# Transposing attention probabilities by DMA from SBUF to SBUF for tiles 6 to 23 of a fused chunk attention and gated feed-forward kernel

## The chip, the cores and the metric

The kernel runs on one core of a Trainium2 chip. The metric is the device time of one execution in microseconds (us), lower is better. The kernel before was timed three times: 257.49, 254.13 and 254.38 us, with a median of 254.38 us. One more execution was recorded by the hardware profiler; it took 255.2 us, and its span from the first to the last instruction is 253.4 us.

## The reference

Chunked attention with a few memory keys, followed by a feed-forward layer with a ReLU gate. Its core, with B = 4 batches, H = 8 heads, S = 768 rows, D = 64:

```python
for c in range(nc):                                  # 24 chunks of 32 query rows
    q_c = q[:, :, c_start:c_end]
    k_full = concat([mem_k, k[:, :, l_start:r_end]]) # 8 memory keys, up to 56 context keys
    v_full = concat([mem_v, v[:, :, l_start:r_end]])
    scores = scale * matmul(q_c, k_full.T)
    a = exp(scores - max(scores))
    a = a / (sum(a) + 1e-09)
    out[:, :, c_start:c_end] = matmul(a, v_full)
x = out.transpose(0, 2, 1, 3).reshape(3072, 512)
y = (maximum(x @ w_gate, 0) * (x @ w_val)) @ w_out    # 512 -> 1536 -> 512
```

## The kernel before

**Tiles.** The 3072 rows are 24 tiles of 128 rows, six to a batch. A tile a passes through a chain of steps, each named by a short key in the planner: `t` transposes the loaded q and k on TensorE into PSUM and `tc` copies them to SBUF; `s` multiplies scores (L239); `max`, `sub`, `exp`, `sum`, `rec`, `nrm` make the probabilities, the last of them writing the SBUF tile `p_n` (L284, VectorE); `p` transposes `p_n` with four TensorE transposes of 128x128 against an identity into the PSUM tile `pT_ps` (L290), and `pc` copies that to the SBUF tile `pT` on ScalarE (L75) or VectorE (L77), whichever the planner finds free; `v` multiplies the transposed probabilities with the values in 16 small matmuls (L303), and `x` copies the result into `xT`, the feed-forward input.

**Blocks.** The feed-forward layer works on blocks of 3, 3, 4, 4, 4, 4 and 2 tiles. For block b it runs 12 steps `f`, each a gate and a value product of four matmuls (L322), with a ReLU on ScalarE (L328) and the product on VectorE (L334), and then, tile by tile, the output products `o` in groups of three matmuls (L343), a copy `oc` to an SBUF tile `o_sb` (three buffers) and a store to HBM, which SyncE issues (L350). A block's first `f` needs `xT` of all its tiles. The attention of the next block's tiles is spread over the `f` and `o` steps of the current block (a function `pace` ties a tile's start to an `f` step).

**What sets the order.** A planner inside the kernel simulates the engines with cost figures of its own, starts on every free engine the ready operation of the best priority, and writes the program in that order. Each engine then executes its instructions strictly in order, so that the order is fixed when the kernel is built and only the waits are decided on the chip. An entry of the planner names the engine and its cost, the operations that must be done (a pair adds a delay), a priority, and the buffers that it takes and gives back.

**SyncE's queue** issues DMAs in order as well: the 24 stores, and, once for each of batches 1 to 3, eight small DMAs that copy the memory rows from SBUF to SBUF (`mem_rows`, L143, 24 KB each). The semaphores of its DMAs are shared round robin by eight, so that each DMA waits until the eighth one before it has landed. GpSimd issues all large loads, with casts, on a queue of its own.

The probabilities' two steps in the planner:

```python
op(("p", a), {"PE": 0.24}, lambda e, a=a: p_t(a), [("nrm", a)], (1, a, 8), ["aps"], ["pn"])
op(("pc", a), psum(HP * 128), lambda e, a=a: p_copy(a, engine[e]), [("p", a)], (1, a, 9), ["pT"], ["aps"])
```

Of the kernel before, what the change touches and what calls it, by code (L numbers as in the profile page):

```python
# [11 lines left out]
F16 = mybir.dt.float16  # L12
# [8 lines left out]
def kernel(  # L21
# [12 lines left out]
    nc = tc.nc  # L34
# [9 lines left out]
    HP = H // 2  # L44
# [8 lines left out]
    EARLY = TPB  # L53
# [7 lines left out]
    smpool = ctx.enter_context(tc.tile_pool(name="smpool", bufs=2))  # L61
# [7 lines left out]
    aps = ctx.enter_context(tc.tile_pool(name="aps", bufs=2, space=bass.MemoryType.PSUM))  # L69
# [3 lines left out]
    def copy(eng, o, i):  # L73
        if eng is nc.scalar:
            nc.scalar.copy(o, i)  # L75
        else:
            eng.tensor_copy(o, i)  # L77
# [126 lines left out]
    P_n, PT, S_ps, SM, TMP = {}, {}, {}, {}, {}  # L204

    def qk_t(a, i):
        ps = TMP["qk", a, i] = aps.tile([128, HP, 128], BF16, tag="aps", name="qk_ps")
        x = qk_b.pop((a, i))
        for hp in range(HP):
            nc.tensor.transpose(ps[:, hp, :], x[:, 2 * hp:2 * hp + 2, :].rearrange("p h d -> p (h d)"), ident_b)  # L210

    def qk_copy(a, i, eng):
        b, t = divmod(a, TPB)
        ps = TMP.pop(("qk", a, i))
        if i == 0:
            copy(eng, qT[b][:, :, 128 * t:128 * t + 128], ps)
        else:
            o = kT[b][:, :, 4 * t:4 * t + 4, :]
            copy(eng,
                 bass.AP(tensor=o.tensor, offset=o.offset,  # L220
                         ap=[o.ap[0], [NCH * KW, HP], [KW, 4], [16 + NMEM, 2], [1, 16]]),
                 ps.rearrange("p h (c x s) -> p h c x s", c=4, x=2))

    def scores(a):
        b, t = divmod(a, TPB)
        s = sps.tile([128, 2, 512], F32, name="s_ps")
        keys = kT[b].rearrange("p h c s -> p h (c s)")
        for h2 in range(HP):
            m, par = h2 % 2, h2 // 2
            for g in range(4):  # L230
                c = 4 * t + g
                o0 = 64 * (2 * m + par)
                for r in range(2):
                    d = slice(D * r, D * r + D)
                    for k0, k1, c0 in KEY_RUNS if a < EARLY else ((0, 64, 0),):
                        k0, k1, c0 = KW * c - 16 + k0, KW * c - 16 + k1, o0 + c0 - (KW * c - 16 + k0)
                        k0, k1 = max(k0, 0), min(k1, NCH * KW)
                        if k0 < k1:
                            nc.tensor.matmul(s[CH * g:CH * g + CH, r, c0 + k0:c0 + k1],  # L239
                                             lhsT=qT[b][d, h2, CH * c:CH * c + CH],  # L240
                                             rhs=keys[d, h2, k0:k1], start=True, stop=True)
        S_ps[a] = s.rearrange("p a (h s) -> p a h s", s=64)[:, :, 0:HP, :]

    def row_max(a):
        t = a % TPB
        s4 = S_ps[a]
        if t == 0:
            nc.vector.memset(s4[0:CH, :, :, 0:16], NEG)
        if t == TPB - 1:
            e = CTX if a < EARLY else 64  # L250
            nc.vector.memset(s4[3 * CH:4 * CH, :, :, e - 8:e], NEG)
        SM[a, "mx"] = smpool.tile([128, 2, HP], F32, name="mx")
        nc.vector.reduce_max(SM[a, "mx"], s4, axis=AX.X)  # L253

    def subtract(a):
        mx = SM.pop((a, "mx"))
        SM[a, "dif"] = smpool.tile([128, 2, HP, 64], F32, name="dif")
        mx_b = bass.AP(tensor=mx.tensor, offset=mx.offset,
                       ap=[mx.ap[0], [HP, 2], [1, HP], [0, 64]])
        ps = S_ps.pop(a)  # L260
        for i0, i1, o0 in KEY_RUNS if a >= EARLY else ((0, 64, 0),):
            nc.vector.tensor_tensor(out=SM[a, "dif"][:, :, :, o0:o0 + i1 - i0], in0=ps[:, :, :, i0:i1],  # L262
                                    in1=mx_b[:, :, :, i0:i1], op=ALU.subtract)

    def exponent(a):
        p = SM[a, "p"] = smpool.tile([128, HP, 2, 64], F16, name="p_exp")
        nc.scalar.activation(p.rearrange("p (m r) a s -> p r m (a s)", r=2),  # L267
                             SM.pop((a, "dif")).rearrange("p r (m a) s -> p r m (a s)", a=2),
                             ACT.Exp, scale=SCALE)

    def row_sum(a):
        SM[a, "sm"] = smpool.tile([128, HP, 2], F32, name="sm")
        nc.vector.reduce_sum(SM[a, "sm"], SM[a, "p"], axis=AX.X)  # L273

    def reciprocal(a):
        SM[a, "rinv"] = smpool.tile([128, HP, 2], F32, name="rinv")
        nc.vector.reciprocal(SM[a, "rinv"], SM.pop((a, "sm")))

    def normalise(a):
# [3 lines left out]
        P_n[a] = smpool.tile([128, HP, 2, 64], F16, name="p_n")  # L283
        nc.vector.tensor_tensor(out=P_n[a], in0=SM.pop((a, "p")), in1=rinv_b, op=ALU.mult)  # L284

    def p_t(a):
        ps = TMP["p", a] = aps.tile([128, HP, 128], F16, tag="aps", name="pT_ps")
        x = P_n.pop(a)
        for hp in range(HP):
            nc.tensor.transpose(ps[:, hp, :], x[:, hp].rearrange("p a s -> p (a s)"), ident_h)  # L290

    def p_copy(a, eng):
        PT[a] = smpool.tile([128, HP, 128], F16, name="pT", bufs=6)
        copy(eng, PT[a], TMP.pop(("p", a)))
# [67 lines left out]
    def op(key, eng, fn, deps=(), prio=(0,), take=(), give=(), after=()):  # L362
        ops[key] = dict(eng=eng, fn=fn, deps=list(deps), prio=prio, take=list(take), give=list(give),
                        after=list(after))
# [4 lines left out]
    def psum(n):  # L369
        return {"ACT": 0.21 + 0.83e-3 * n, "DVE": 0.22 + 1.04e-3 * n}  # L370

    engine = {"ACT": nc.scalar, "DVE": nc.vector}
# [22 lines left out]
    def pace(a):  # L395
        blk = block_of[a]
        return [("f", blk - 1, NDC * (a - starts[blk]) // BLOCKS[blk], 0)] if blk > 1 else []

    for a in range(NT):
        b, t = divmod(a, TPB)  # L400
        last = t == TPB - 1
        for i in (1, 0):
            op(("t", a, i), {"PE": 0.24}, lambda e, a=a, i=i: qk_t(a, i), [("qk", a, i), "ib", ("new", b)],
               (1, a - i, 0), ["aps"], ["qk"], pace(max(a - i, 0)))
            op(("tc", a, i), psum(HP * 128), lambda e, a=a, i=i: qk_copy(a, i, engine[e]), [("t", a, i)],
               (1, a - i, 0), (), ["aps"])
        op(("s", a), {"PE": 0.8 if a < EARLY else 0.36}, lambda e, a=a: scores(a),
           [("tc", a, 0), ("tc", a, 1)] + ([] if last else [("tc", a + 1, 1)]), (1, a, 1), ["sps"],
           ["kv"] if last else [], [("s", a - 1)] if a else [])
        op(("max", a), {"DVE": 0.74 + (0.2 if t == 0 or last else 0)}, lambda e, a=a: row_max(a), [("s", a)],  # L410
           (1, a, 2), ["mx"])
        op(("sub", a), {"DVE": 0.74 if a < EARLY else 1.2}, lambda e, a=a: subtract(a), [("max", a)],
           (1, a, 3), ["dif"], ["sps", "mx"])
        op(("exp", a), {"ACT": 0.66}, lambda e, a=a: exponent(a), [("sub", a)], (1, a, 4), ["p"], ["dif"])
        op(("sum", a), {"DVE": 0.74}, lambda e, a=a: row_sum(a), [("exp", a)], (1, a, 5), ["sm"])
        op(("rec", a), {"DVE": 0.24}, lambda e, a=a: reciprocal(a), [("sum", a)], (1, a, 6), ["rinv"], ["sm"])
        op(("nrm", a), {"DVE": 0.74}, lambda e, a=a: normalise(a), [("rec", a)], (1, a, 7), ["pn"], ["p", "rinv"])
        op(("p", a), {"PE": 0.24}, lambda e, a=a: p_t(a), [("nrm", a)], (1, a, 8), ["aps"], ["pn"])
        op(("pc", a), psum(HP * 128), lambda e, a=a: p_copy(a, engine[e]), [("p", a)], (1, a, 9), ["pT"], ["aps"])
        blk = block_of[a]  # L420
        j = a - starts[blk]
        op(("v", a), {"PE": 0.45}, lambda e, a=a: values(a),
           [("pc", a)] + [("vl", b, 0 if b else t // 3, n) for n in range(2 if b else 2 * HP)]
           + ([("mr", b)] if b else []), (1, a, 10), ["aps"] + (["xT"] if j == 0 else []), ["pT"],
           [("v", a - 1)] if a else [])
        op(("x", a), psum(HP * 128), lambda e, a=a: x_copy(a, engine[e]), [("v", a)], (1, a, 11), (), ["aps"],
           [("x", a - 1)] if a else [])
# [6 lines left out]
    for rank, (blk, m) in enumerate(seq):  # L434
        n = BLOCKS[blk]
# [212 lines left out]
```

## Time and profile before

| What | us | Where it is read |
|---|---|---|
| median of three runs | 254.38 | times |
| profiled execution, its span | 255.2, 253.4 | times, page |
| PE busy, of the span | 231.7 (91%) | page, part 1 |
| `f` products of value and gate, busy | 76.2 and 76.5 | page, part 5, L322 |
| output products, busy | 66.1 | page, part 5, L343 |
| probability transposes, 96 of them for 24 tiles, busy | 10.3 | groups by line, L290 |
| copies of `pT`: 15 on ScalarE of 0.585, 9 on VectorE of 0.424 | 8.8 and 3.8 | groups by line, L75 and L77 |
| first gate product of blocks 2, 3, 4, 5, 6 starts at | 89.70, 126.62, 163.52, 200.27, 233.96 | chain that ended last |

A busy figure of PE adds overlapping matmuls with modelled ends; how much of PE's line an operation takes is better read from the chain, where one piece starts when the one before it leaves the engine. The granted TensorE clock is 0.999 over the span. The DMA engines carry GpSimd's loads until about 130 us (the DMA row of the slices is at 9 there) and are almost idle later, but for the stores.

### The profile page before, as it was taken

The page shows a single profiled execution, that of the slowest core. Times are in us where ns is not written, and L with a number is a line of the kernel's source. Part 1 is how long each engine was busy: PE and PEld are TensorE (multiplying, and loading weights), DVE is VectorE, ACT ScalarE, POOL GpSimd, SP SyncE. Part 2 cuts the span into 40 slices and gives each one's busy share as a digit, 9 for nine tenths or more (in the row PEclk, how much of TensorE's full clock was granted, in tenths as well). Part 3 has the DMA queues.
Part 4 walks back from the last instruction along what each step waited for, and adds up shares of the span by engine and source line. Part 5 has one row for each costly group of instructions (what it writes and reads, how often), then busy time and mean ns, then how long its engine had stood idle before and what let it go on. Part 6 is the DMA issues. An engine that isn't in the chain of part 4 may idle for free.

```text
span 253.4 us, 6546 instructions
## 1 busy us (share of the span) xinstructions
PE 231.7 (91%) x2785; PEld 129.9 (51%) x2785; DVE 142.0 (56%) x295; ACT 107.1 (42%) x197; POOL 89.7 (35%) x102
## 2 busy tenths in 40 slices
PE   1628777999999999999999999999999999999993
PEld 0417555666654544554545555544545545454861
DVE  3957664567764247775257775168774075810430
ACT  3426444445454244543253554354434434332421
POOL 8999699993335644597010000000000000000000
PEclk9999999999999999999999999999999999999999
DMA  8999999999999999999991001210002200002102
GB/s 63 113 113 132 164 148 175 160 144 192 145 151 158 201 180 151 152 136 109 181 192 23 0 3 41 87 41 3 3 1 83 85 0 3 0 27 101 41 3 83
DMA packets 115053, 23.99 MB, mean 95 GB/s; under 512 B 106320, under 2 KB 111952, under 8 KB 115024
## 3 DMA queue, kind: packets, MB, share of 16 engines
q0 software_dynamic: 106400, 16.61, 89.2%
q1 hardware_dynamic: 8624, 6.97, 9.7%
q8 instruction: 22, 0.36, 0.6%
q14 instruction: 7, 0.06, 0.1%
HBM read 33.24 MB, written 6.29 MB: 156 GB/s over the span
## 4 chain that ended last, share of the span: by engine, by line
PE 77%; POOL 9%; DMA 8%; SPq 2%; issue 2%; ACT 1%; POOLq 0%; ACTq 0%
PE v_ps L322 24%; PE g_ps L322 24%; PE out_ps L343 21%; POOL v_bd L167 4%; POOL qk_b L189 4%; PE qk_ps L210 3%; DMA w_val_sb<-in_moe_w_val_dram 3%; DMA w_gate_sb<-in_moe_w_gate_dram 3%; PE xT_ps L303 2%; DMA out_dram<-o_sb 2%; SPq L143 2%; PE s_ps L239 2%; PE pT_ps L290 1%; POOL w_gate_sb L101 0%; ACT o_sb L75 0%
## 5 line engine op out<-in xcount | busy, mean ns | idle before, releaser
L322 PE MATMUL v_ps<-xT,w_val_sb 128*128 128x512 f16 (+2 forms) x336 | 76.2, 349 | 0.9 <-DMA w_val_sb<-in_moe_w_val_dram 0.9
L322 PE MATMUL g_ps<-xT,w_gate_sb 128*128 128x512 f16 (+2 forms) x336 | 76.5, 351 | 0.3 <-ACT xT L75 0.3
L328 ACT ACTIVATE g_relu<-g_ps 128x512 f16<-128x512 f32 (+2 forms) x84 | 45.0, 536 | 73.2 <-PE g_ps L322 63.7
L334 DVE TENSOR_TENSOR gvT<-v_ps,g_relu 128x512 f16<-128x512 f32 (+2 forms) x84 | 51.6, 614 | 42.7 <-PE v_ps L322 29.3
L343 PE MATMUL out_ps<-w_out_sb,gvT 128*128 128x512 f16 x288 | 66.1, 379 | 0.0
L322 PEld LDWEIGHTS <-w_gate_sb 128*128 128x128 f16 x336 | 32.5, 98 | 29.2 <-issue 1.2
L322 PEld LDWEIGHTS <-w_val_sb 128*128 128x128 f16 x336 | 30.6, 98 | 22.9 <-issue 1.4
L343 PEld LDWEIGHTS <-gvT 128*128 128x128 f16 x288 | 26.8, 98 | 28.7
L167 POOL DMA_DIRECT2D v_bd<-in_v_dram x24 | 27.9, 1182 | 11.3 <-issue 8.7
L75 ACT COPY o_sb<-out_ps 128x512 f32<-128x512 f32 x24 | 14.1, 586 | 34.3 <-PE out_ps L343 31.0
L189 POOL DMA_DIRECT2D qk_b<-in_k_dram x24 | 22.8, 949 | 14.9 <-PE v_ps L322 4.0
L210 PE MATMUL qk_ps<-ident_b,qk_b 128*128 128x128 bf16 x192 | 19.9, 241 | 8.2 <-DMA qk_b<-in_q_dram 6.1
L189 POOL DMA_DIRECT2D qk_b<-in_q_dram x24 | 22.5, 940 | 13.0 <-PE qk_ps L210 9.0
L210 PEld LDWEIGHTS <-qk_b 128*128 128x128 bf16 x192 | 14.2, 106 | 13.2 <-DMA qk_b<-in_q_dram 6.7
L273 DVE TENSOR_REDUCE sm<-p_exp 128x8 f32<-128x512 f16 x24 | 16.3, 679 | 7.6 <-ACT p_exp L267 7.4
L253 DVE TENSOR_REDUCE mx<-s_ps 128x8 f32<-128x512 f32 x24 | 16.4, 685 | 7.2 <-PE s_ps L239 6.9
L262 DVE TENSOR_TENSOR dif<-s_ps,mx 128x256 f32<-128x256 f32 (+3 forms) x60 | 18.7, 362 | 0.2
L267 ACT ACTIVATE p_exp<-dif 128x512 f16<-128x512 f32 x24 | 15.2, 632 | 4.8 <-DVE dif L262 4.7
L284 DVE TENSOR_TENSOR p_n<-p_exp,rinv 128x512 f16<-128x512 f16 x24 | 16.5, 687 | 0.4
L77 DVE COPY qT<-qk_ps 128x512 bf16<-128x512 bf16 x9 | 3.8, 424 | 21.2 <-PE qk_ps L210 21.2
L303 PEld LDWEIGHTS <-v_bd 128*128 128x128 f16 x384 | 12.9, 97 | 4.4 <-issue 0.8
L75 ACT CAST xT<-xT_ps 128x512 f16<-128x512 f32 x18 | 10.5, 586 | 9.4 <-PE xT_ps L303 9.3
(37 smaller groups left out, 126.4 us busy)
## 6 DMA issues: line engine op xcount, KB each, us to landing
out_dram<-o_sb SPq DMA_DIRECT2D x24, 256.0 KB
v_bd<-in_v_dram POOLq DMA_DIRECT2D x5, 672.0 KB, 16.3
qk_b<-in_k_dram POOLq DMA_DIRECT2D x24, 128.0 KB, 8.0
qk_b<-in_q_dram POOLq DMA_DIRECT2D x24, 128.0 KB, 7.5
w_gate_sb<-in_moe_w_gate_dram POOLq DMA_DIRECT2D x8, 192.0 KB, 6.1
w_val_sb<-in_moe_w_val_dram POOLq DMA_DIRECT2D x8, 192.0 KB, 6.7
w_out_sb<-in_moe_w_out_dram POOLq DMA_DIRECT2D x2, 768.0 KB, 11.7
v_bd<-in_v_dram POOLq DMA_DIRECT2D x15, 84.0 KB, 4.7
```

The lines of the kernel that those rows point to most:

```text
L75: nc.scalar.copy(o, i)
L167: nc.gpsimd.dma_start(dst[64 * par + s0:64 * par + s1, c0:c1, D * par:D * par + D], bass.AP(tensor=v.tensor, offset=v[b, HP * par, 0, 0].o ...
L189: nc.gpsimd.dma_start(qk_b[a, i], bass.AP(tensor=x.tensor, offset=x[b, 0, 128 * t, 0].offset, ap=[[D, 128], [S * D, H], [1, D]]))
L210: nc.tensor.transpose(ps[:, hp, :], x[:, 2 * hp:2 * hp + 2, :].rearrange("p h d -> p (h d)"), ident_b)
L253: nc.vector.reduce_max(SM[a, "mx"], s4, axis=AX.X)
L262: nc.vector.tensor_tensor(out=SM[a, "dif"][:, :, :, o0:o0 + i1 - i0], in0=ps[:, :, :, i0:i1], in1=mx_b[:, :, :, i0:i1], op=ALU.subtract)
L284: nc.vector.tensor_tensor(out=P_n[a], in0=SM.pop((a, "p")), in1=rinv_b, op=ALU.mult)
L303: nc.tensor.matmul(ps[:, hp, r], lhsT=v_bd[b % NSET][:, hp, 4 * t + g, :], rhs=x[:, hp, r], start=True, stop=True)
L322: nc.tensor.matmul(ps, lhsT=w[:, f, 128 * m:128 * m + 128], rhs=xTs[blk][:, f, :], start=(f == 0), stop=(f == NFC - 1))
L328: nc.scalar.activation(st["r", m], st.pop((0, m)), ACT.Relu)
L334: nc.vector.tensor_tensor(out=st["gv"][:, m, :], in0=st.pop((1, m)), in1=st.pop(("r", m)), op=ALU.mult)
L343: nc.tensor.matmul(st["o", t], lhsT=st["gv"][:, m, 128 * t:128 * t + 128], rhs=w_out_sb[:, m, :], start=(m == 0), stop=(m == NDC - 1))
```

## The change

For tiles 6 to 23 the two steps are replaced by one, `pc` on SyncE's queue: four DMAs with transposition, each from one 128x128 quarter of `p_n` to the same quarter of `pT`. Tiles 0 to 5 (`EARLY` is 6) keep TensorE and the copy. The planner is given 3.0 us of SyncE's time for the four and a delay of 2.5 us before `v`. The PSUM buffer `pT_ps` is no longer taken by these tiles, and `p_n` is held until the DMAs are done.

```diff
+    def p_dma(a):
+        PT[a] = smpool.tile([128, HP, 128], F16, name="pT", bufs=6)
+        x = P_n.pop(a)
+        for hp in range(HP):
+            nc.sync.dma_start(PT[a][:, hp, :], x[:, hp].rearrange("p a s -> p (a s)"), transpose=True)
+
...
-        op(("p", a), {"PE": 0.24}, lambda e, a=a: p_t(a), [("nrm", a)], (1, a, 8), ["aps"], ["pn"])
-        op(("pc", a), psum(HP * 128), lambda e, a=a: p_copy(a, engine[e]), [("p", a)], (1, a, 9), ["pT"], ["aps"])
+        if a < EARLY:
+            op(("p", a), {"PE": 0.24}, lambda e, a=a: p_t(a), [("nrm", a)], (1, a, 8), ["aps"], ["pn"])
+            op(("pc", a), psum(HP * 128), lambda e, a=a: p_copy(a, engine[e]), [("p", a)], (1, a, 9), ["pT"], ["aps"])
+        else:
+            op(("pc", a), {"SP": 3.0}, lambda e, a=a: p_dma(a), [("nrm", a)], (1, a, 8), ["pT"], ["pn"])
...
-           [("pc", a)] + [("vl", b, 0 if b else t // 3, n) for n in range(2 if b else 2 * HP)]
+           [("pc", a) if a < EARLY else (("pc", a), 2.5)] + [("vl", b, 0 if b else t // 3, n) for n in range(2 if b else 2 * HP)]
```

Since the planner decides the order of all engines, the new costs move other instructions too.

## The prediction

> **What bounds the kernel now.** The page comes first: who is busy, and which chain ended last.
>
> ```profile
> PE 231.7 (91%) x2785; PEld 129.9 (51%) x2785; DVE 142.0 (56%) x295; ACT 107.1 (42%) x197; POOL 89.7 (35%) x102
> ...
> PE 77%; POOL 9%; DMA 8%; SPq 2%; issue 2%; ACT 1%; POOLq 0%; ACTq 0%
> ```
>
> Three quarters of the chain are PE, the rest mostly the loads of the first 40 us. The busy times by stretch, cut at the first gate product of each block, show how full PE is (columns: stretch, length, then busy us of PE, PEld, DVE, ACT, POOL, the clock, DMA share, GB/s):
>
> ```profile
> 90.00:126.60 36.60, 36.60 (x384) 18.62 (x383) 23.03 (x50) 15.19 (x28) 19.56 (x18) 1.00 2.11 150
> 126.60:163.50 36.90, 36.88 (x386) 18.98 (x385) 22.48 (x48) 16.81 (x30) 0.87 (x1) 1.00 0.40 60
> ```
>
> PE has no free time here, at the full clock, so only what leaves PE's line can shorten these stretches, and any wait of PE lengthens them. The eighteen copies that go were ScalarE's and VectorE's, busy 15 to 23 us of 37: no gain. The timeline at the end of block 2, with tile 13, the last one block 3 needs:
>
> ```profile
> 114.58 0.31 PE L239 MATMUL s_ps<-kT,qT 64*32 64x64 bf16 x32
> ...
> 114.82 3.41 PE L343 MATMUL out_ps<-w_out_sb,gvT 128*128 128x512 f16 x15
> ...
> 121.43 0.68 DVE L284 TENSOR_TENSOR p_n<-p_exp,rinv 128x512 f16<-128x512 f16 x1
> 123.22 0.39 PE L290 MATMUL pT_ps<-ident_h,p_n 128*128 128x128 f16 x4
> ...
> 123.45 2.11 PE L343 MATMUL out_ps<-w_out_sb,gvT 128*128 128x512 f16 x9
> ...
> 125.39 0.56 PE L303 MATMUL xT_ps<-pT,v_bd 128*128 128x32 f16 x16
> 125.79 0.81 PE L343 MATMUL out_ps<-w_out_sb,gvT 128*128 128x512 f16 x3
> 125.98 0.59 ACT L75 CAST xT<-xT_ps 128x512 f16<-128x512 f32 x1 [1.97 <-PE xT_ps L303]
> 126.62 0.59 PE L322 MATMUL g_ps<-xT,w_gate_sb 128*128 128x512 f16 x2
> ```
>
> Read start against start: four transposes hold PE from 123.22 to 123.45, 0.23 us; `v` holds it 0.40; from the end of `v` to the gate product that needs its copy, 126.62 - 125.79 = 0.83 us pass, and three output matmuls (0.65) cover them.
>
> The third place is SyncE's queue, the transposes' new home. The timeline of that queue, the chain after it, the durations of its two kinds of issue (min, median, max in ns) and its wait at the very end:
>
> ```profile
> 51.78 11.26 SPq L143 DMA_DIRECT2D v_bd<-vmem  x8
> ```
> ```profile
> 75.23 7.31 SPq L143 DMA_DIRECT2D v_bd<-vmem  x8
> ```
> ```profile
> 82.64 5.84 DMA out_dram<-o_sb
> ...
> 88.58 0.59 ACT o_sb L75
> 89.16 0.50 ACT xT L75
> ...
> 89.70 1.02 PE g_ps L322 x4
> ```
> ```profile
> L143 SPq DMA_DIRECT2D v_bd<-vmem x24: 685/718/3779, 51.8 to 134.0; - x24
> ```
> ```profile
> L350 SPq DMA_DIRECT2D out_dram<-o_sb x24: 332/333/519, 74.7 to 250.3; - x24
> ```
> ```profile
> SPq L643 <- DMA out_dram<-o_sb: 1.4, 1, 1.4
> ```
>
> A store issued at 82.64, beside the loads, lands at 88.48: 5.4 us after its 0.48 of issue. The last store, beside nothing, lands 1.4 us after its issue. Block 2 already starts late through this queue.
>
> **What leaves PE.** 18 tiles x 0.23 = 4.1 us. That is the whole possible gain: 1.6% of the profiled 255.2 us. About 2%, 5.1 us, is what a measurement of this kernel can tell from no change, so even the full gain would be below it.
>
> **What the new order takes back.** In the built program of the changed kernel `v` of tiles 9, 13, 17 and 21, the last of their blocks, is PE's last work before the next block's gate product; the three matmuls that stood behind it are ahead of it. So the copy's 0.83 us are bare, once for each of blocks 2 to 5. Against the four transposes saved per block (0.92), a block gains 0.1. Only the last two tiles keep theirs, 0.45.
>
> **What a DMA transpose costs.** No row shows one. The leg from `p_n` to `v` is L = 4i + r + 0.1, with i the issue of one on SyncE, r the landing, 0.1 the signal. For i the nearest rows are the store, 0.33 (128 partitions, 2 KB each), and the memory rows, also SBUF to SBUF in small pieces, 0.72 at the median; under the heaviest load eight of these took 11.26, 1.41 each. I take 0.70, the small-piece row, with 0.33 and 1.41 as ends. For r the ends are 1.4 and 5.4; with the DMA engines idle (after 130 us, tile 14 on) I take 1.4, beside the loads (tiles 8 to 13) the middle, 3.4. So L is 4.3 late and 6.3 early.
>
> [...]
>
> **What L may be.** PE work between `s` and `v` of a tile in the changed order, less the time that the chain from `s` to the end of `p_n` takes now, is free for L:
> - Tile 13: 16 groups of three output matmuls (0.648) and two `v`: 11.2, less 122.11 - 114.82 = 7.3: 3.9 us.
> - Tile 21, the same work, less 194.14 - 188.49 = 5.6: 5.5 us. Tile 17: two `f` and a `v` more, 13.3 less 6.7: 6.6 us.
> - The others from tile 10 on, with 12.7 to 19 us of work ahead and chains of 6 to 9.3: 5.1 (tile 20) to about 11 (tile 14), mostly 7. Tiles 6 and 7 wait over 15 us for `v` already.
> - `p_n` has two buffers, now held for L instead of the transposes' 0.2: the next but one `nrm` on VectorE waits for it only where two tiles come within L; inside a block they are over 6 us apart (p_n at 100.8, 107.3, 116.0, 121.4), so this costs nothing while L stays below that.
>
> **Block 2.** Tiles 8 and 9 go behind the memory rows, which leave SyncE at 82.54. The order there is: store, store, tile 8's four, store, tile 9's four. By issue alone tile 9 is out at 82.54 + 0.9 + 2.8 + 0.5 + 2.8 = 89.5. But the second of its four shares the semaphore of the store issued at 82.64, and waits for its landing at 88.48: 88.5 + 3 x 0.70 = 90.6. Landing 3.4 and signal 0.1: 94.1. `v` and the bare copy, 1.23: block 2 starts at 95.3, not 89.70: +5.6. Between the ends of i and r: +2.5 to +9.7. Queued behind these DMAs are two more stores, whose `o_sb` buffers ScalarE waits for; they come in the same stretch.
>
> **The sum.** Block 2 +5.6; block 3: tile 13 exceeds its room by 6.3 - 3.9 = 2.4, less 0.1: +2.3; blocks 4 and 5, L 4.3 below 5.1: -0.1 each; the last two tiles -0.45. Together +7.3 us: 255.2 + 7.3 = 262.5 for a profiled execution, which stood 0.8 above the median, so 262 as a time. With both low ends it is 2.5 - 0.3 - 0.45 = +1.8. With both high ends, L 11.1 early and 7.1 late: block 2 +9.7, tiles 10 to 12 some 4, tile 13 some 7, tiles 16 to 22 together some 6, less 0.8: +26.
>
> **Rivals.**
> - Likeliest, 0.42: i between 0.5 and 1.05, as summed: 260 to 266 us.
> - Not slower (0.29): the transposes do not queue behind the loads, r stays 1.4 at tiles 8 to 13. Then with i = 0.70 block 2 starts at 88.5 + 2.1 + 1.5 + 1.23 = 93.3, +3.6, tile 13 is 0.4 over, and the sum is +3.3; with i = 0.33 it is +1.8: 256 to 258 us. It decides below r = 2.3, where +3.3 + 2 x 0.9 reaches 5.1. For it: SBUF-to-SBUF, no HBM at either end. Against: the same 16 engines carry GpSimd's loads, and the memory rows' max of 3.78 us is such a queue.
> - The transposes' issue is SyncE's bound (0.27): i from 1.05 to 1.41 and above. Then L is over 5.7 even late, tiles 20 and 21 and then others wait too, each us of L costs several: 266 to 281 us. For it: a transposing DMA is many small pieces. Against: with engines idle no row of SyncE reaches it.
> - Faster by over 2% (0.02): 4.1 us is all there is on PE.
> - That the change does not do what it says is excluded: the built program has 72 transposing DMAs on SyncE, and PE 144 rows fewer.
>
> **Numbers.** The likeliest gives 262 us. The range takes in all three, 255 to 281, leaving about 0.07 above (a slower i) and 0.05 below. Slower by over 2% (259.5): the third and most of the first, 0.66; within 2%: the second and the edge of the first, 0.32; faster 0.02.
>
> **What will show it.** The issue rows of the transposes on SyncE give i at once; waits of `xT_ps` on `pT`'s DMAs, and their place, give L against its room: at tiles 9 and 13 alone if I am right, at inner tiles if the third rival is, nearly none if the second. Every block's first gate product should wait about 0.8 us for its `xT` copy. I am wrong if blocks 4 and 5 lengthen beyond 37 us, or if block 2 starts before 92 us.

## The result and the profile after

The changed kernel takes 287.69 us (median of 4 runs, 285.02 to 288.75) beside 255.94 for the kernel before (4 runs, 254.13 to 257.72): a ratio of 1.127, 95% interval 1.121 to 1.133. It is slower, as forecast, but 26 us slower than the forecast and 7 us outside the range. Here and below a time is the median of all executions, while a ratio leaves out those that took over 1.5% longer than the fastest of the same kernel. The profiled execution took 288.75 with a span of 286.9, against 255.2 and 253.4 before. The page of the changed kernel, its busy times, the granted clock over the span, and the chain that ended last:

```profile
PE 239.5 (83%) x2713; PEld 130.2 (45%) x2713; DVE 136.8 (48%) x282; ACT 105.1 (37%) x192; POOL 89.9 (31%) x102
...
PEclk9999988999999558999957899999999999999999
...
PE 69%; DMA 11%; SPq 8%; POOL 4%; issue 3%; ACT 3%; DVE 1%; DVEq 0%; ACTq 0%; POOLq 0%
```

Two things are to be seen. SyncE's queue and DMAs have grown to a fifth of the chain. And PE is busy 7.8 us longer than before with 72 rows fewer; the clock line has two holes, down to 5 tenths, and the longer busy time lies in the stretches with these holes. Mean granted clock: 0.940, before 0.999. The stretches from one block's first gate product to the next (stretch, length, busy us of PE, PEld, DVE, ACT, POOL, clock, DMA share, GB/s; the first row is the lateness of block 2):

```profile
89.70:103.80 14.10, 2.77 (x35) 1.59 (x34) 1.69 (x2) 2.25 (x4) 7.07 (x5) 0.59 1.78 160
103.80:155.50 51.70, 41.25 (x368) 19.68 (x368) 21.67 (x47) 15.48 (x27) 14.68 (x14) 0.86 1.60 111
155.50:196.50 41.00, 38.83 (x369) 19.09 (x369) 21.05 (x45) 16.34 (x29) 0.88 (x1) 0.94 0.20 42
```

Before, blocks 2 to 6 began at 89.70, 126.62, 163.52, 200.27 and 233.96; now at 103.83, 155.50, 196.47, 234.07 and 267.47. So the 33.5 us by which the span grew are: 14.1 ahead of block 2, 14.8 in block 2 (51.7 for 36.9), 4.1 in block 3, 0.9 in block 4, -0.3 in block 5, nothing after it. Of the 14.1 not all is the change's: block 1's first gate product is already 2.5 us late, before and after,

```profile
53.08 0.65 PE g_ps L322 x4
```
```profile
55.62 0.65 PE g_ps L328 x4
```

although PE's instructions have the same order in both kernels up to here and the first transposing DMA is issued at 64.3. In the other runs below, block 1 starts between 1 us earlier and 2 us later than before, so this is a difference between executions. 11.6 of the 14.1 belong to the change. PE's own waits name the cause (total us, times, longest):

```profile
PE xT_ps L309 <- DMA pT<-p_n: 22.4, 15, 5.7
...
PE g_ps L328 <- ACT xT L75: 2.7, 4, 0.7
```

The second row is the bare copy, four times 0.67 us. The first is the transposing DMA. The longest of its waits are not only at the last tiles of a block: tile 8 waits 6.0 us in four pieces and tile 12 7.0 in two, beside 4.7 at tile 9 and 2.7 at tile 13. The longest piece of tile 8's and of tile 12's in the timeline (in brackets the wait):

```profile
94.16 0.29 PE L309 MATMUL xT_ps<-pT,v_bd 128*128 128x32 f16 x4 [3.88 <-DMA pT<-p_n]
```
```profile
145.78 0.27 PE L309 MATMUL xT_ps<-pT,v_bd 128*128 128x32 f16 x4 [5.65 <-DMA pT<-p_n]
```

What SyncE pays to issue one (min, median, max in ns; first and last start):

```profile
L290 SPq DMA_TRANSPOSE pT<-p_n x72: 1093/1230/3105, 64.3 to 258.4; - x72
```

Not 0.70 us but 1.23, and never below 1.09. The chain at tile 9, ahead of block 2 (start, length, what):

```profile
92.02 1.10 SPq L290
...
95.89 6.95 DMA pT<-p_n
102.89 0.28 PE xT_ps L309 x4
103.19 0.59 ACT xT L75
103.83 1.87 PE g_ps L328 x4
```

Tile 9's four issues take SyncE from 92.02 to 97.13, 5.1 us, as tile 8's did before them (86.17 to 91.29). The last lands at 102.84, 5.7 us after its issue. Then come `v`, the bare copy, and a gate product that takes 1.87 us where it took 1.02 before. The same chain at tiles 12 and 13, ahead of block 3:

```profile
132.13 0.61 DVE p_n L284
132.79 1.09 SPq L290
...
135.21 3.10 SPq L290
138.36 2.83 SPq L290
...
142.80 2.63 SPq L290
...
146.75 7.50 DMA pT<-p_n
154.30 0.55 PE xT_ps L309 x8
...
155.50 1.87 PE g_ps L328 x4
```

`p_n` of tile 12 is ready at 132.7 and that of tile 13 at 136.9, 4.2 us later, less than four issues take. Some issues take 2.6 to 3.1 us here, and two stores stand between. So tile 13 waits 5.9 us for its first issue, and its leg from `p_n` to the last landing is 17.3 us; it had been given 6.3, and had 3.9 of room. What else happens there shows on GpSimd's queue: the value loads of batch 3, in the timeline after and then before (`no_v_loads` below tests whether they are the reason),

```profile
132.63 4.97 POOL L167 DMA_DIRECT2D v_bd<-in_v_dram  x3 [10.82 <-PE xT_ps L309]
```
```profile
112.31 2.21 POOL L167 DMA_DIRECT2D v_bd<-in_v_dram  x1 [0.26 <-PE qk_ps L210]
```

These loads wait until `v` of tile 11 frees their buffer (the bracket: 10.82 us of idling, ended by `xT_ps`). `v(11)` does not wait for its transposes; it ends 28.3 us after block 2's first gate product instead of 22.1, since the new order has it later, and block 2 starts 14 us late. So the loads are issued at 132.6 instead of 112.3, 0.16 us ahead of tile 12's transposes.

The clock holes lie at and behind the two long waits:

```profile
90.30:103.80 13.50, 2.19 (x32) 1.50 (x33) 1.69 (x2) 2.25 (x4) 6.91 (x5) 0.58 1.83 160
103.80:109.40 5.60, 5.57 (x20) 2.48 (x19) 1.12 (x2) 1.18 (x2) 1.20 (x2) 0.50 2.56 147
```

PE idles for most of 13.5 us, and the next 5.6 us, in which it never waits, run at half clock, 2.8 us lost; from 109.4 on it is 1.00 again. Behind block 3's wait the same goes from 155.5 to 160.6, some 2.5 us.

### The profile page after: what moved, and what is told of

Read it like the earlier page. It is cut to its first block, busy times and chain, and to the rows that moved or that the text cites. A ratio compares the mean times of both kernels' runs of the same rounds, so it can differ in the third digit from the quotient of the medians.

```text
span 286.9 us, 6498 instructions
## 1 busy us (share of the span) xinstructions
PE 239.5 (83%) x2713; PEld 130.2 (45%) x2713; DVE 136.8 (48%) x282; ACT 105.1 (37%) x192; POOL 89.9 (31%) x102
## 3 DMA queue, kind: packets, MB, share of 16 engines
q1 hardware_dynamic: 20144, 9.33, 13.9%
## 4 chain that ended last, share of the span: by engine, by line
PE 69%; DMA 11%; SPq 8%; POOL 4%; issue 3%; ACT 3%; DVE 1%; DVEq 0%; ACTq 0%; POOLq 0%
PE g_ps L328 24%; PE v_ps L328 23%; PE out_ps L349 13%; SPq L290 8%; DMA pT<-p_n 7%; PE qk_ps L210 4%; PE s_ps L239 3%; POOL qk_b L189 2%; PE xT_ps L309 2%; DMA out_dram<-o_sb 2%; DMA qk_b<-in_q_dram 2%; POOL v_bd L167 1%; ACT xT L75 1%; ACT o_sb L75 1%; PE pT_ps L296 1%
## 5 line engine op out<-in xcount | busy, mean ns | idle before, releaser
L328 PE MATMUL g_ps<-xT,w_gate_sb 128*128 128x512 f16 (+2 forms) x336 | 80.3, 363 | 4.0 <-ACT xT L75 2.7
L328 PE MATMUL v_ps<-xT,w_val_sb 128*128 128x512 f16 (+2 forms) x336 | 78.5, 357 | 0.0
L328 PEld LDWEIGHTS <-w_gate_sb 128*128 128x128 f16 x336 | 33.2, 101 | 32.5 <-issue 7.3
L328 PEld LDWEIGHTS <-w_val_sb 128*128 128x128 f16 x336 | 31.8, 100 | 24.4 <-issue 1.8
L349 PEld LDWEIGHTS <-gvT 128*128 128x128 f16 x288 | 27.5, 99 | 31.8 <-issue 1.9
L309 PE MATMUL xT_ps<-pT,v_bd 128*128 128x32 f16 x384 | 16.0, 180 | 23.2 <-DMA pT<-p_n 22.4
L75 ACT COPY o_sb<-out_ps 128x512 f32<-128x512 f32 x24 | 14.1, 586 | 42.4 <-PE out_ps L349 35.6
L309 PEld LDWEIGHTS <-v_bd 128*128 128x128 f16 x384 | 14.1, 98 | 29.1 <-issue 17.2
L75 ACT CAST xT<-xT_ps 128x512 f16<-128x512 f32 x20 | 11.7, 586 | 35.1 <-PE xT_ps L309 35.0
L210 PEld LDWEIGHTS <-qk_b 128*128 128x128 bf16 x192 | 15.2, 111 | 15.7 <-DMA qk_b<-in_q_dram 6.7
L273 DVE TENSOR_REDUCE sm<-p_exp 128x8 f32<-128x512 f16 x24 | 16.3, 680 | 10.4 <-ACT p_exp L267 10.3
```

The source lines that it names most:

```text
L309: nc.tensor.matmul(ps[:, hp, r], lhsT=v_bd[b % NSET][:, hp, 4 * t + g, :], rhs=x[:, hp, r], start=True, stop=True)
L328: nc.tensor.matmul(ps, lhsT=w[:, f, 128 * m:128 * m + 128], rhs=xTs[blk][:, f, :], start=(f == 0), stop=(f == NFC - 1))
L349: nc.tensor.matmul(st["o", t], lhsT=st["gv"][:, m, 128 * t:128 * t + 128], rhs=w_out_sb[:, m, :], start=(m == 0), stop=(m == NDC - 1))
```

## The experiments

The theory after this result, A: the price is SyncE's issue of 1.23 us per DMA, and the rest follows from it, since (so I thought) block 2's lateness moves GpSimd's loads onto tiles 12 and 13. Its rivals, B: the landing beside loads (5 to 6 us) is the price, whatever the issue; C: the order of stores and transposes in SyncE's queue; D: the planner, which reserves 3.0 us of SyncE and a delay of 2.5 for a leg that takes 6 and more, puts `v` too early on PE; E: the clock. Ratios are to the kernel before, run on the same chip, whose medians were 255.3 to 256.6 us. Every diff is against the changed kernel, and `...` stands for lines left out.

**Which tiles cost it.** `late_only` leaves tiles 6 to 13 to TensorE, `early_only` tiles 14 to 23:

```diff
-        if a < EARLY:
+        if a < 14:                      # late_only
+        if a < EARLY or a >= 14:        # early_only
```

> DMA transposes for tiles 14 to 23 alone; 6 to 13 go back to TensorE and a copy. If the loss comes from the early tiles, whose transposes land behind GpSimd's loads (and from the clock that falls in the waits they cause), blocks 2 and 3 start where they did before and only some 3 us are left: 256 to 260 us, clock 1.0. If the issue of 1.23 us each on SyncE is what costs, loaded or not, ten of eighteen tiles keep their share, some 18 of 33 us: about 273.

> The other part: DMA transposes for tiles 6 to 13, TensorE for 14 to 23. If the early tiles are the loss: 282 to 288 us, block 2 about 14 late, block 3 about 29, nothing added behind it. If the issue is the loss in every tile: about 15 us, 270.

`late_only`: 261.89 us, ratio 1.028 (0.995 to 1.060), between the two times expected. Blocks 2 and 3 start nearly as before, at 90.95 and 127.87; block 3 takes 40.3 us, since tile 17 waits 3.1, and block 4 38.6, whose first 4.2 us have a granted clock of 0.59. `early_only`: 284.41, ratio 1.116 (1.083 to 1.149), blocks 2 and 3 at 103.43 and 153.84. So most of the loss comes with tiles 6 to 13, those beside GpSimd's loads; the ten late ones cost some 5 us, an amount that the interval does not tell from nothing, and gain nothing, although little but the stores is on the DMA engines there (42, 37 and 44 GB/s in blocks 3, 4 and 5 of the changed kernel, 111 in block 2). Tile 17 in the changed kernel shows why:

```profile
189.47 1.11 SPq L290
...
193.18 2.33 DMA pT<-p_n
195.55 0.27 PE xT_ps L309 x4
```

Less the issue of 1.23 the last DMA lands in 1.1 us. But the first of the four goes out 1.9 us after `p_n` is ready (187.6), behind tile 16's and two stores, and four issues then make the leg long enough for PE to stand there.

**Issue or landing.** `half` sends only two of the four quarters through DMAs, the others through TensorE and a copy of half the size; `halves` cuts every DMA into two of 64 rows; `one_dma` sends all four quarters in one:

```diff
-        for hp in range(HP):
+        for hp in range(2):             # half, and for the other two:
...
+            nc.tensor.transpose(ps[:, hp, :], x[:, 2 + hp].rearrange("p a s -> p (a s)"), ident_h)
...
+        copy(eng, PT[a][:, 2:4, :], TMP.pop(("p", a)))
...
-            nc.sync.dma_start(PT[a][:, hp, :], x[:, hp].rearrange("p a s -> p (a s)"), transpose=True)
+            for r in (0, 64):           # halves
+                nc.sync.dma_start(PT[a][:, hp, r:r + 64], x[r:r + 64, hp].rearrange("p a s -> p (a s)"), transpose=True)
+        nc.sync.dma_start(PT[a], x.rearrange("p h a s -> p (h a s)"), transpose=True)   # one_dma
```

> Of each tile from 6 on, two quarters go by DMA and two by TensorE and a copy of half the size. The leg has two issues less, 2.5 us; the landing behind the loads is the same. If the issues carry the loss, block 2 starts some 7 us earlier than with four (tiles 8 and 9 stand one behind the other) and block 3 some 10 to 14: 262 to 268 us. If the landing behind the loads carries it, with 5.8 us whatever the number, less is won: 275 to 280.

> Each transposing DMA is cut into two of 64 rows, so a tile has eight. If the issue of 1.23 us goes with the size, eight take about as long as four did, and the time is 287 to 297. If it is a cost of each DMA, whatever its size, a tile takes 9.8 us of SyncE, and eighteen tiles add about 5 us each to the leg, most of it bare: over 340.

> One transposing DMA for the whole tile (128 rows of 512) in place of four of 128 columns. If the issue's 1.23 us is a price of each DMA, whatever its size, a tile takes 1.2 us of SyncE instead of 4.9, and the loss falls to some 10 to 20 us, what the landing behind the loads and the bare copies cost: 265 to 275. If it is a price of each 128x128 block, one DMA holds SyncE about as long as four: 285 to 290.

`half`: 277.91 us, 1.091 (1.058 to 1.123), on the landing's side of what was expected: block 2 starts at 95.89, 8 us earlier than with four (5.2 earlier counted from block 1's first gate product, near the four issues of 1.23 saved at tiles 8 and 9), but its stretch is still 50.6 us. `halves`: 371.26 (one run); PE waits 76.3 us for `pT` in 55 waits. `one_dma`: 273.20, 1.066 (1.058 to 1.074). The issue rows of the last two, `halves` first:

```profile
L291 SPq DMA_TRANSPOSE pT<-p_n x144: 1089/1226/3831, 62.2 to 339.2; - x144
```
```profile
L289 SPq DMA_TRANSPOSE pT<-p_n x18: 1189/1196/3480, 62.0 to 238.8; - x18
```

Half the rows, 1.23 us; one quarter, 1.23 (above); four quarters, 1.20. For these three sizes the issue is a price per DMA and not per byte, row or 128x128 block. With it cut to a quarter, 14.5 us come back (287.69 - 273.20), but almost 18 stay (273.20 beside 255.43). A is right about a part of block 2's delay: counted from block 1, block 2 starts 6.2 us earlier, about half of the 11.6. The rest is there with one issue too, as tile 9's single DMA shows, 1.3 us of issue and 6.5 of landing, and so does tile 13's, which takes 11 us, 3.5 of issue and 7.6 of landing:

```profile
86.14 7.74 DMA pT<-p_n
...
129.46 11.05 DMA pT<-p_n
140.56 0.62 PE xT_ps L308 x16
```

It also shows that the lateness of block 2 is not what brings the loads to tile 13: block 2 starts 8.6 us earlier here, the loads go out at 124.3 and 126.5, and tile 13's DMA still meets them. They are released by `v(11)`, just ahead of tile 12's `p_n` in this order, wherever the block begins.

**The loads.** `no_v_loads` leaves out the four value loads of batches 2 and 3 (tiles 12 to 23 then use old values); `v_loads_later` was to hold them back until `v` of tiles 9 and 13:

```diff
-            load_v_op(b, 0, par, 0, HP * NCH, par, [], deps)
+            if b < NSET:                # no_v_loads
+                load_v_op(b, 0, par, 0, HP * NCH, par, [], deps)
+            else:
+                load(("vl", b, 0, par), 0, 0.0, lambda: None, [], (), deps)
+            load_v_op(b, 0, par, 0, HP * NCH, par, [("v", {2: 9, 3: 13}[b])] if b >= NSET else [], deps)   # v_loads_later
```

> The changed kernel without GpSimd's four large loads of values for batches 2 and 3 (672 KB each; the values of batches 0 and 1 stay in their place, so the output of tiles 12 to 23 is other than the reference). In the changed kernel two of them are issued when tile 9's transposes go out and two with tile 12's. If the transposes' landing queues behind these, tiles 12 and 13 land some 2 us after their issue instead of 4.6 to 6.2, the stretch of block 2 falls from 51.7 us to about 40, and block 2 starts some 3 us earlier: 268 to 275 us in all. If a transpose's landing is long early for another reason (the number in flight, SyncE's own stores and memory rows): over 282.

> The same four loads are kept but issued later: for batch 2 after tile 9's values, for batch 3 after tile 13's. If it is a matter of which transfers lie before the transposes in time, tile 13's leg shortens as without the loads, and block 2's stretch falls by about 10 us; batch 2's loads may now meet tiles 10 and 11, whose room is 7 us: 272 to 280. If the loads are no cause: 285 to 290.

`no_v_loads`: 275.03 us, 1.079 (1.056 to 1.100). Block 2 starts at 101.55, hardly earlier, but its stretch falls from 51.7 to 41.2, and tile 13's last DMA goes as a late one does:

```profile
138.15 1.23 SPq L290
139.43 2.38 DMA pT<-p_n
```

No issue of tiles 12 and 13 takes over 1.3 us, and the last lands 1.15 after its own: the loads were what made both slow at tiles 12 and 13. Tile 9's landing stays slow, 5.4 us after its last issue, beside GpSimd's loads of q and k, which are still there. `v_loads_later` says nothing: 287.71 us, 1.128 (1.112 to 1.145), because the edit moved only a time in the planner; GpSimd's queue kept its order and issued batch 3's loads at 132.6 as before.

With the loads left out on top of `one_dma`:

> One DMA for a tile and no large loads of values for batches 2 and 3 (output of tiles 12 to 23 other than the reference, as before). If the number of DMAs and these loads are separate prices, both gains show, 14.5 and 12.7 of 33 us: 259 to 263, with block 3 starting 37 us after block 2, and what is left is tiles 8 and 9 behind SyncE's memory rows and stores. If they are one and the same wait seen twice: 268 to 273.

263.53 us, 1.034 (1.027 to 1.041). The two prices add up nearly: 14.5 and 12.7 us apart, 24.2 together. The time is just above the 259 to 263 expected, and block 3 starts 38.5 us after block 2, not 37. Of the 8 us that are left, 6.5 are ahead of block 2 (96.25 for 89.70), where tile 9's DMA goes out at 86.42, 6.3 us after `p_n`, behind the memory rows and stores, and lands 8.5 us later, 7.2 after its issue. So B's price, the landing beside loads, is what is left there, with the place in the queue.

**The order on SyncE.** `stores_act` lets ScalarE issue the output's stores:

```diff
-        nc.sync.dma_start(out[row:row + 128, :], o)
+        nc.scalar.dma_start(out[row:row + 128, :], o)
```

> The 24 stores are issued by ScalarE instead of SyncE, so tile 9's transposes stand behind tile 8's alone and share no semaphores with stores. If waiting in SyncE's queue carries part of the loss, block 2 starts 3 to 4 us earlier, tile 13's transposes go out 1.5 us earlier, tile 17's and 21's 1 us: 280 to 284. If the queue's order costs nothing: 286 to 289, or more, since ScalarE now issues and waits.

290.31 us, 1.139 (1.117 to 1.160): no gain. The eight issues of tiles 8 and 9 start at 86.94, right behind the memory rows, which end later here; the first of tile 9 starts at 93.15 (92.02 before the edit), though no store of the queue stands ahead of it, and block 2 at 108.0. The chain holds a wait that the changed kernel did not have:

```profile
93.99 6.03 DMA out_dram<-o_sb
...
100.04 6.97 DMA pT<-p_n
```

Tile 9's last DMA, which could have started at 96.8, is held until a store of ScalarE's has landed at 100.02, 3.2 us. That is the kind of wait that I had forecast for SyncE's store. Without it block 2 would have started at about 104.8, no earlier than the 103.83 of the changed kernel, whose block 1 had begun 2 us later. So this run has nothing for C: moving the stores out of the queue does not bring tile 9 out sooner.

**The planner.** `planner_told` gives it 5.0 us of SyncE for a tile and a delay of 6.0 (1.5 from tile 14 on):

```diff
-            op(("pc", a), {"SP": 3.0}, lambda e, a=a: p_dma(a), [("nrm", a)], (1, a, 8), ["pT"], ["pn"])
+            op(("pc", a), {"SP": 5.0}, lambda e, a=a: p_dma(a), [("nrm", a)], (1, a, 8), ["pT"], ["pn"])
...
-            [("pc", a) if a < EARLY else (("pc", a), 2.5)] + [("vl", b, 0 if b else t // 3, n) for n in range(2 if b else 2 * HP)]
+            [("pc", a) if a < EARLY else (("pc", a), (1.5 if a >= 14 else 6.0))] + [("vl", b, 0 if b else t // 3, n) for n in range(2 if b else 2 * HP)]
...
```

> Four DMAs as in the change, but the planner is told what they take: 5.0 us of SyncE, and 1.5 us of delay before the values late, 6.0 early. If the loss came from the planner's too small figures (3.0 and 2.5), which place the values ahead of their data, it puts other work there and the time falls to 265 to 275. If the work to fill the time with is not there, since the last tile of a block is needed by the next block's first product, it only moves the waits: 283 to 290.

285.68 us, 1.115 (1.106 to 1.123), and PE still waits 24.1 us for `pT`. D is worth some 2 us, and its interval touches the changed kernel's (1.121 to 1.133): telling the planner the measured leg does not remove the waits.

**The clock.** `filler` puts 81 gate-shaped matmuls on PE around the waits of tiles 8, 9, 12 and 13, some between the quarters of `v`, so the earlier quarters of these four tiles are overwritten. `one_filler` does it for `one_dma`, 51 matmuls ahead of the first quarter:

```diff
+    FILL = {8: (16, 4, 3, 0), 9: (10, 3, 3, 2), 12: (24, 5, 0, 0), 13: (4, 7, 0, 0)}   # filler, ahead of quarter hp
...
+            for _ in range(FILL.get(a, (0, 0, 0, 0))[hp]):
...
+        for _ in range({8: 13, 9: 10, 13: 28}.get(a, 0)):                               # one_filler
+            nc.tensor.matmul(ps.rearrange("p h s -> p (h s)"), lhsT=w_gate_sb[:, 0, 0:128], rhs=w_val_sb[:, 0, 0:512],
+                             start=True, stop=True)
```

> The changed kernel with 81 more matmuls, of 0.22 us each, in the places where TensorE waits for the transposes of tiles 8, 9, 12 and 13 (into the PSUM tile that the values then overwrite; their results are not used). They fill the waits and are no longer than these. If the fall of the granted clock after the waits is a cost of its own, it stays at 1.0, the first products of blocks 2 and 3 take 0.86 instead of 1.87, and some 5 us are won: 281 to 284. If the clock does not hang on TensorE's idling, or costs nothing, the time stays at 286 to 289 or grows.

> One DMA for a tile, and 51 more matmuls of 0.22 us ahead of the values of tiles 8, 9 and 13, where TensorE waits for 3.1, 2.5 and 6.6 us; the values overwrite what they write. If the clock falls because TensorE idles there, it stays at 1.0, block 3's stretch falls from 39.5 to 37 us, and the time from 273 to 269 to 271. If the clock falls for another reason: 273 or more, with the clock down about 10 us after tile 13's wait as before.

`filler`: 291.45 us, 1.144 (1.105 to 1.182). The clock stays at 1.0 as far as 195 us and block 3's stretch falls from 41.0 to 38.8, but block 2's does not (52.8), since tile 13's transposes, which land at 152.8 and later as in the changed kernel, set its end and not PE. Later blocks lose: block 4 takes 40.5 for 37.6, and begins with 3.5 us at a granted clock of 0.51. On the total it decides nothing. `one_filler`: 270.21, 1.061 (1.054 to 1.067), beside 273.20 (1.058 to 1.074): the intervals overlap, and the reading rests on the windows. The first 5.6 us of block 3, in `one_dma` and then in `one_filler`:

```profile
141.80:147.40 5.60, 5.56 (x20) 2.47 (x19) 1.12 (x2) 1.18 (x2) 0.88 (x1) 0.50 1.72 146
```
```profile
141.80:147.40 5.60, 5.60 (x63) 2.76 (x63) 3.08 (x7) 1.98 (x4) 0.88 (x1) 1.00 1.91 159
```

Both start the block at 141.8. With PE kept busy through its wait, these 5.6 us hold 63 matmuls instead of 20, at the full clock, and the block takes 36.8 us instead of 39.5. So E is a part of the loss: this wait of PE costs its length and then 2.8 us more.

**A version without waits.** If the explanation holds, DMA transposes where the leg has room, with tiles 17 and 21 left to TensorE, must keep TensorE's saving and lose nothing. `inner_late` has four DMAs a tile for tiles 14 to 23 without 17 and 21, `one_inner` one DMA for the inner tiles from 6 on, `one_room` one DMA for tiles 10, 11 and the late inner ones; in each the planner is told the measured leg:

```diff
-        if a < EARLY:
+        if a < 14 or a in (17, 21):                         # inner_late, SP 5.0, delay 1.5
+        if a < EARLY or a in (8, 9, 12, 13, 17, 21):        # one_inner, SP 2.0, delay 5.0, from tile 14 on 2.0
+        if a < 10 or a in (12, 13, 17, 21):                 # one_room, SP 2.0, delay 2.0
...
```

> The four DMAs only where the profile has room for them: tiles 14 to 23 without 17 and 21, which end a block; the planner is told 5.0 and 1.5 us. Eight tiles x 0.23 us leave TensorE, no wait of it for a transpose should be over 0.5 us, no block waits for a bare copy: 1 to 2 us faster than before, ratio 0.992 to 0.998. If a transposing DMA disturbs TensorE's work otherwise, or the room is too small, the ratio is over 1.

> One DMA for a tile, and only where there is room: tiles 6, 7, 10, 11, 14, 15, 16, 18, 19, 20, 22 and 23; TensorE for those that end a block, and for 8 and 12, which go out beside the large loads. The planner is told 2.0 us of SyncE, and 5.0 (early) or 2.0 of delay. If a transpose in the room is free, 12 x 0.23 us leave TensorE: 2 to 3 us faster than before, ratio 0.988 to 0.993. If tiles 10 and 11 meet loads and wait, or planning moves more than it saves: 0.995 or more.

> One DMA for a tile, for tiles 10, 11, 14, 15, 16, 18, 19, 20, 22 and 23; tiles 6 and 7 are back on TensorE, so that the order up to block 2's first product is that of the kernel before. If the order around the stores was what cost 4 us there, block 2 starts at about 89.7 as before and ten tiles save 0.23 each: ratio 0.985 to 0.995, blocks 2, 3 and 4 about 36.1 us each. If the transposes of tiles 10 and 11 cost what the others save: 0.997 or more.

`inner_late`: 254.36 us (10 runs), ratio 0.995 (0.990 to 0.999): faster than the kernel before by half a per cent, with an interval that just leaves out 1. The trace shows where. PE waits for no `pT` at all, and blocks 3 and 4 take 36.1 us where they took 36.90 and 36.75; block 3:

```profile
126.60:162.70 36.10, 36.08 (x373) 18.14 (x372) 21.75 (x46) 16.34 (x29) 0.88 (x1) 1.00 0.46 72
```

The two blocks together gain 1.5 us for six tiles, 0.25 a tile. `one_inner`: 257.57, 1.010 (1.004 to 1.016), a miss: the later blocks take 36.3, 36.1 and 36.1, but block 2 starts at 94.05. Its chain there:

```profile
83.11 5.80 DMA out_dram<-o_sb
89.02 0.59 ACT o_sb L75
...
90.14 0.58 PE xT_ps L308 x16
```

With other costs in its plan the planner put a copy into `o_sb` on ScalarE, which waits 5.6 us for a store to land, ahead of two copies of `xT`, one of which PE then waits 3.0 us for. `one_room`, in which block 2 starts at 88.96, removes that loss but not more: 256.69 (12 runs), 0.995 (0.990 to 1.001), not told from no change. Tile 10, beside loads, waits 1.8 us, and the clock falls after it (the 3.4 us around the wait, then the next 3.4):

```profile
105.70:109.10 3.40, 1.61 (x23) 0.78 (x21) 1.63 (x5) 1.13 (x2) 0.00 (x0) 1.00 2.46 125
109.10:112.50 3.40, 3.40 (x16) 1.76 (x15) 1.42 (x4) 1.27 (x4) 3.07 (x4) 0.51 3.02 128
```

So block 2 takes 39.9 us instead of 36.9 and loses more than the 2.0 us that blocks 3 to 5 win.

## Why the forecast was wrong

- **The step that failed first is "What a DMA transpose costs".** I took i = 0.70 from the memory rows as small pieces between SBUF and SBUF; it measures 1.23, nearly four store issues. `halves` and `one_dma` show that it is a price per DMA. The third rival had i right, 1.05 to 1.41, at a chance of 0.27; its time, up to 281 us, was still too low. The many small pieces that it went by are there, 160 packets of some 205 bytes for each of the 72 DMAs (the hardware queue carried 20,144 packets and 9.33 MB, before 8,624 and 6.97), but the issue did not follow the size. The argument against it, that with engines idle no row of SyncE reached it, was no evidence: SyncE had issued no such DMA. With no load beside them issue and landing together take 2.3 us (tile 17): the landing, 1.1, is near the last store's 1.4, the issue, 1.23, far from a store's 0.33. The prediction's own sum with the measured 1.23, and with landings of 5.7 early and 1.1 late, gives +19 for the tiles that it charged, an estimate (block 2 +11.1, tile 13 +6.7, tiles 20 and 21 +1.4, the last two -0.45); the other 13 to 15 of the measured 32 to 33.5 us lie in the steps below and in the 2.5 us ahead of block 1.
- **r was right late and too low early.** 1.1 to 1.2 at most of the late DMAs for the 1.4 taken; early 5.7 at tile 9 and 6.2 at tile 13, above the upper end of 5.4, where I took the middle of two ends.
- **"What L may be" and "The sum" treated each tile's leg by itself.** Even with i = 1.23 and r = 5.4, L of tile 13 is 10.4; it was 17.3. Two things were left out. Four issues (4.9 us) are longer than the 4.2 between `p_n` of tiles 12 and 13, so SyncE is a queue there. And the loads of batch 3, released by `v(11)`, hold up the issue itself at these tiles; `no_v_loads` shows all that the value loads cost, 12.7 us. The late block did not bring them there, as `one_dma` shows; before the change, too, they were issued at 112.3 and 114.9, and `p_n` of tiles 12 and 13 ended at 116.7 and 122.1. Waits were expected at tiles 9 and 13 alone, yet tiles 8 and 12 waited longest. And the line "inside a block they are over 6 us apart" does not hold even before: its own figures 116.0 and 121.4 are 5.4 apart.
- **The clock was not in the sum.** The waits ahead of blocks 2 and 3 cost 2.8 and some 2.5 us after they had ended.
- **"Block 2" had the right place for a wrong reason.** The shared semaphore of the store, which was to hold tile 9's second issue until 88.5, never bound there: the store landed at 90.67, and that issue started at 93.17. Four issues each for tiles 8 and 9 did, 10.2 us instead of 5.6, and the landing; 2.0 us more come from the memory rows, which left SyncE at 84.54 for 82.54, with block 1's later start. The upper end of +9.7 was also summed wrongly: at i = 1.41 the queue itself takes until 82.54 + 0.9 + 5.6 + 0.5 + 5.6 = 95.2, later than the semaphore's 92.7, which makes +12.2 and the top of the range 2.5 us higher, still below the result.
- **Right:** the sign; 0.23 us a tile as the whole gain (0.25 in `inner_late`); no free time on PE, so that each wait lengthened its block; the bare copy, 0.67 each for 0.83; no gain to be seen from ScalarE's and VectorE's copies; enough room at the late inner tiles, which wait for nothing, in the changed kernel and in `inner_late`. Tiles 17 and 21 did wait, 1.5 and 0.65 us; the third rival had late waits, but named tiles 20 and 21. And block 4 took 37.6 us, over the 37 that was given as a sign of being wrong.

What stays open: why the clock fell behind tile 17's wait of 1.5 us in `filler` and not behind the same wait in the changed kernel; where the 2.5 us ahead of block 1 come from; and how much of the 12.7 us in `no_v_loads` is the held-up issue and how much the landing, which no run parts.

## What to carry to other kernels

Before work is moved to DMAs, price the issue on the queue that gets it, per DMA, and add up the whole queue, not one leg; put as much into one DMA as its shape allows (here 18 for 72: 14.5 us). Where an engine has no free time, only consumers with room to spare may be fed by the longer path: eight tiles so chosen gained half a per cent, all eighteen lost 13. Read, too, which transfers of other queues are released close to the new ones: here the value loads that wait for `v(11)` went out just ahead of tile 12's transposes and slowed both their issue and their landing.

## What the runs showed of the hardware

- Issuing a transposing DMA took SyncE 1.20 to 1.23 us at the median for 64x128, 128x128 and 128x512 elements alike, against 0.33 for a store of 128x512.
- Behind GpSimd's value loads, issued from 132.6 to 137.6 in the changed kernel, three issues of tiles 12 and 13 on SyncE took 2.6 to 3.1 us, and tile 13's in `one_dma` 3.5; with these loads left out none at the two tiles was above 1.3. Beside loads the last transpose of a tile landed 5.7 us (tile 9) and 7.6 us (tile 13 of `one_dma`) after its issue, alone mostly 1.1. Six of the 40 of tiles 14 to 23 in the changed kernel landed later without loads too, 1.9 to 3.0 after their issue, and four of these 40 issues took 1.6 to 2.4.
- Two long waits of TensorE were followed by half clock: in the changed kernel ahead of block 2 (busy for 2.19 of 13.5 us) and in `one_dma` ahead of block 3 (0.61 of 7.8), with 0.50 granted for the next 5.6 us, of which PE was busy for 5.56 or more, before it returned to 1.00. In `one_room` the same came behind a shorter one: PE idled for 1.8 of 3.4 us, and the next 3.4 us ran at 0.51. `one_filler`, with the waits filled, kept 1.00.
